# Attention and an MLP on one core: a Newton step and a scaling given to GpSimd, with a new table of half slots

## The chip, the core and the metric

The kernel runs on one core of a Trainium2 chip. The core has a matrix engine (PE; PEld is its loading of weights), two engines for elementwise work that read the matrix engine's result banks (VectorE, called DVE, and ScalarE, called ACT), GpSimd (POOL), which works on the on-chip memory SBUF alone, and SyncE (SP), which issues the transfers here. Each engine takes its instructions strictly in the order in which they were written for it. The metric is device microseconds (us) of one execution; of several runs the median counts.

## What is computed

Attention of 8 batches, 12 heads, 448 positions and 64 channels, with q and k normalised first, and behind it an MLP with exp(h) − 1 for negative h:

```python
q_n, k_n = (rmsnorm(q, g_q), rmsnorm(k, g_k))      # x / sqrt(mean(x*x) + 1e-6) * g
scores = scale * np.matmul(q_n, k_n.transpose(0, 1, 3, 2))
scores = scores - np.max(scores, axis=-1, keepdims=True)
attn = np.exp(scores)
attn = attn / (np.sum(attn, axis=-1, keepdims=True) + 1e-09)
out = np.matmul(attn, v)                           # (8, 12, 448, 64)
x = out.transpose(0, 2, 1, 3).reshape(3584, 768)
h = x @ w_in                                       # 768 -> 2048
g = np.where(h > 0.0, h, np.exp(np.minimum(h, 0.0)) - 1.0)
y = g @ w_out                                      # 2048 -> 768
```

## The kernel before

**Tiles.** Two heads make a pair: 48 pairs, six to a batch. A pair has 896 rows of scores, seven tiles of 128 rows, 336 tiles in all. Matrix products run in 16-bit halves: a number is split into a high and a low part, and two or three products are added in one bank. The weights are converted inside the kernel, in the first two batches: w_in in 16 pieces (`conv_in`), w_out in 24 (`conv_out`). In both, DVE joins bits (L243) and puts the sign back (L267), ACT makes two copies (L237, L238) and a high part (L327), POOL scales (L291, L322) and subtracts (L331).

**The way of q and k of a pair.** `load_qk`, `qk_square` (ACT, L372), `qk_sum` (DVE, L376), `qk_root` (ACT, L380 and L381: r0 = exp(−0.5 ln(mean))), `qk_newton` (DVE, lines 384 to 393 of the source: one Newton step that sharpens r0, four instructions on 14 columns that the trace has on L387 twice, L388 and L391), `qk_norm` (POOL, L401), the split into halves (ACT L410 and L420, POOL L424 and L431), and transfers that transpose it.

**The way of a tile.** `s_mm` (PE, L554) writes the scores into a bank; `s_max` (DVE, L561); `s_exp` (ACT, L575), with the sum as by-product; `s_z` (POOL, L579), one column: adds the small constant to the sum; `s_rec` (DVE, L587), its reciprocal; `s_hi` (ACT, L618, or L612) and `s_lo` (DVE, L628, or L625) write both halves of the weights of the values; then a transfer, or for the pairs 1, 3 and 5 a product with a diagonal (POOL L591, PE L599), turns them. The banks of scores are used in a ring of five, later of four, so `s_mm` waits until `s_lo` of an earlier tile is done.

**The MLP.** `mlp` yields one matrix product after the other (first layer L743, second layer L757). Behind the 18 products of one of 16 blocks of h, `m1_out` finishes the block in five steps, one slot apart: `one` (ACT, L682, exp of the bank), `two` (ACT, L686, e·isc − isc), `three` (DVE, L690, minimum and maximum against the bank), `four` (ACT, L695) and `five` (DVE, L698), which write the two halves of g.

**What sets the order.** The order on every engine is written out by the program: time is cut into slots h, two to a tile, and the table `SCHED` says in which slot (or half slot) each step of each pair, weight piece, batch and tile is written. The row "rate" says how many products of the MLP have been written by slot 85, 92, 99 and so on. Pairs from the twelfth on repeat the last row; so do batches.

Of the kernel before, what the change touches and what calls it, by code (L numbers as in the profile page):

```python
# [13 lines left out]
AF = mybir.ActivationFunctionType  # L14
ALU = mybir.AluOpType
# [4 lines left out]
B, H, S, D = 8, 12, 448, 64  # L20
# [3 lines left out]
NJ = 2 * S // 128  # L24
# [8 lines left out]
def tile_attention_then_elu_mlp(ctx: ExitStack, tc: tile.TileContext, qk, v, v_scan, gg, w_in, w_out, out):  # L33
# [13 lines left out]
    nc = tc.nc  # L47
# [19 lines left out]
    def t_mo():  # L67
# [10 lines left out]
        out=neg, in0=ident, scalar1=-1.0, scalar2=None, op0=ALU.mult  # L78
# [3 lines left out]
        out=ident, in0=ident, scalar1=2.0**UP, scalar2=None, op0=ALU.mult  # L82
# [103 lines left out]
    kap = const.tile([128, 1], F32, name="kap")  # L186
# [196 lines left out]

    def qk_newton(p):
        ss, r0 = st1[p]
        for x, op0, op1 in ((D * 1e-6, ALU.add, ALU.mult), (-0.5 / D, ALU.mult, ALU.mult)):
            nc.vector.scalar_tensor_tensor(out=ss, in0=ss, scalar=x, in1=r0, op0=op0, op1=op1)  # L387
        nc.vector.scalar_tensor_tensor(  # L388
            out=r0, in0=ss, scalar=1.5, in1=r0, op0=ALU.add, op1=ALU.mult
        )  # L390
        nc.vector.tensor_scalar(  # L391
            out=r0[:, NJ:], in0=r0[:, NJ:], scalar1=kap, scalar2=None, op0=ALU.mult
        )
# [171 lines left out]
    def by_pe(T):  # L565


        return T // NJ in PE_PAIRS
# [19 lines left out]

    def s_diag(T):
        dg = dgs[T] = pool.tile([128, 128], F32, tag="dgz", name="dgz", bufs=2)  # L590
        (nc.vector if DIAG_DVE else nc.gpsimd).tensor_scalar(  # L591
            out=dg, in0=ident, scalar1=stats[T][:, 2:3], scalar2=0.0, op0=ALU.mult, op1=ALU.add
        )

# [78 lines left out]
    def m1_out(b, f, ph):  # L673

        sc, isc, nisc, gsc = (t[:, f : f + 1] for t in mscale[b][:4])
        e = None
        g = gts[f]

        def one():
            nonlocal e  # L680
            e = pool.tile([128, S], F32, tag="e", name="e", bufs=3)
            nc.scalar.activation(e, ph[:, :S], AF.Exp, scale=sc)  # L682

        def two():

            nc.scalar.activation(e, e, AF.Identity, scale=isc, bias=nisc)  # L686

        def three():

            nc.vector.scalar_tensor_tensor(  # L690
                out=e, in0=e, scalar=0.0, in1=ph[:, :S], op0=ALU.min, op1=ALU.max
            )

        def four():
            nc.scalar.activation(g[:, 0], e, AF.Copy, scale=gsc)  # L695

        def five():
            nc.vector.scalar_tensor_tensor(  # L698
                out=g[:, 1], in0=e, scalar=gsc, in1=g[:, 0], op0=ALU.mult, op1=ALU.subtract
            )  # L700

        return [one, two, three, four, five]
# [79 lines left out]
    def put(hs, steps):  # L782
        for h, (fn, *args) in zip(hs, steps, strict=True):
            at(h, fn, *args)

    at(-18, gains)
    for T in reversed(range(NCHUNK)):
        k = 2 if by_pe(T) else 0 if T < PB else 1
        hs = [2 * T + h for h in SCHED["tile"][k]]
        j = T % NJ  # L790
        if k < 2:
            put(hs[:6], [(fn, T) for fn in (s_max, s_exp, s_z, s_rec, s_hi, s_lo)])


            at(hs[7 if j == 0 else 8 if j == NJ - 1 else 6], s_tr, T)
        else:
            put(hs, [(fn, T) for fn in (s_max, s_exp, s_z, s_rec, s_diag, s_pe, s_hi, s_lo)])
    for p in range(NP):
        k = p if p < 12 else 11
        put([h + HP * (p - k) for h in SCHED["qk"][k]], [  # L800
# [8 lines left out]
    for b in range(B):  # L809
        k = min(b, 2)  # L810
        hs = [h + HB * (b - k) for h in SCHED["scan"][k]]
# [7 lines left out]
    for b in range(B):  # L819
        k = min(b, 1)  # L820
        hs = [h + HB * (b - k) for h in SCHED["m"][k]]
# [22 lines left out]
    for h in range(H0, LAST):  # L844
        T, odd = divmod(h, 2)
# [9 lines left out]
        p, r = divmod(h, HP)  # L855
# [23 lines left out]
    for h in range(h + 1, h + 9):  # L879
# [3 lines left out]

SCHED = {
# [13 lines left out]
    ],  # L898
    "v": [
        [-2, 14, 15, 17, 18, 23, 24],  # L900
        [17, 23, 24, 24, 26, 36, 37],
        [26, 37, 38, 38, 40, 50, 51],
        [41, 52, 53, 54, 55, 65, 65],
        [54, 65, 66, 68, 68, 78, 79],
        [68, 79, 80, 82, 82, 93, 93],
        [82, 93, 94, 96, 96, 106, 106],
        [96, 107, 109, 109, 110, 120, 121],
        [110, 121, 122, 123, 124, 134, 135],
        [124, 135, 136, 137, 138, 147.5, 148.5],
        [138, 149, 150, 151, 152, 162, 162],  # L910
        [152.5, 163.5, 164.5, 165.5, 166.5, 176.5, 177.5],
    ],
    "scan": [
# [3 lines left out]
    ],  # L917
# [17 lines left out]
    ],  # L935
# [25 lines left out]
    ],  # L961
    "m": [
        [68, 69, 70, 72, 73, 74, 75, 77],
        [153, 154, 155, 156, 158, 159, 160.5, 161.5],
    ],
    "tile": [
# [3 lines left out]
    ],  # L970
    "rate": [
        [4, 8, 46, 104, 148, 188, 240, 288, 336, 382, 430, 478, 536, 576],
    ],
}
WO_OWN = 7

CK = S // 4
PE_PAIRS = (1, 3, 5)
DIAG_DVE = False

RATE_FROM = 85
UP = 13
# [38 lines left out]
```

## Time and profile before

| what | value |
|---|---|
| median of 3 runs | 1270.25 us (1269.4 to 1272.03) |
| the profiled execution's own time | 1268.82 us |
| its span, first to last instruction | 1267.0 us |
| PE busy | 1196.3 us (94%) |
| DVE busy | 861.1 us (68%) |
| ACT busy | 880.6 us (70%) |
| POOL busy | 535.4 us (42%) |

Busy time is the time in which an engine has at least one instruction in work. The shares are means over a kernel with different stages, so the table alone does not say what bounds it: the page's 40 slices (31.7 us each) show PE at 3 to 8 tenths in the first seven slices and at 9 or more from the eighth on, and DVE at 7 to 9 or more in the first eight and at 5 to 8 in most of the later ones. A wait row names who waited, for whom, for how long in total, how often, and the longest.

### The profile page before, as it was taken

Reading aid. Unit: us, or ns where it says so; the run is one execution under the profiler, and the core shown is the slowest. Engines: PE = TensorE matmul, PEld = TensorE weight load, DVE = VectorE, ACT = ScalarE, POOL = GpSimd, SP = SyncE. Lnnn points to the kernel's source line nnn. Section 1 sums busy time; section 2 is a strip of 40 time slices with the busy share of each in tenths; the row PEclk is TensorE's granted clock in tenths of the full one; section 3 lists DMA queues with packets and bytes.
Section 4 is the critical chain, followed back from the end, with each engine's and each line's share of the span. In section 5 each row is a group of like instructions: output and inputs, shape, how many; then the busy total and the mean of one; then the engine's idle time right before and its main releaser. Section 6 shows DMA issues by size and latency. Waiting matters only on the chain.

```text
span 1267.0 us, 21793 instructions
## 1 busy us (share of the span) xinstructions
PE 1196.3 (94%) x7150; PEld 735.0 (58%) x7150; DVE 861.1 (68%) x1913; ACT 880.6 (70%) x1889; POOL 535.4 (42%) x858
## 2 busy tenths in 40 slices
PE   3778678999999999999999999999999999999998
PEld 2435444567556665576556755666557755676576
DVE  7888999986676567755785667756876677642310
ACT  6888789975797568855896578756886579643520
POOL 4766877664434343433434433334334333320000
PEclk9889799999999999999999999999999999999999
DMA  9967799999677986689577976798677968672012
GB/s 296 252 154 188 197 205 201 221 215 227 155 160 151 218 177 156 145 195 215 137 162 160 237 149 158 153 220 186 144 154 184 223 140 157 137 156 76 1 49 63
DMA packets 432979, 214.44 MB, mean 169 GB/s; under 512 B 389089, under 2 KB 409185, under 8 KB 432865
## 3 DMA queue, kind: packets, MB, share of 16 engines
q1 hardware_dynamic: 432864, 213.04, 74.1%
q8 instruction: 57, 0.93, 0.3%
q14 instruction: 58, 0.47, 0.1%
HBM read 93.52 MB, written 14.16 MB: 85 GB/s over the span
## 4 chain that ended last, share of the span: by engine, by line
PE 82%; DVE 10%; ACT 3%; POOL 3%; issue 1%; DMA 1%; SPq 0%; ACTq 0%; POOLq 0%
PE m L757 23%; PE m L743 20%; PE s L757 11%; PE s L743 10%; PE s L554 9%; PE av L658 7%; DVE w32s L267 2%; DVE st L561 1%; DVE wts L243 1%; DVE gall L698 1%; DVE p L628 1%; DVE ss L376 1%; DMA raws<-in_w_out 1%; PE s L599 1%; PE m L298 1%
## 5 line engine op out<-in xcount | busy, mean ns | idle before, releaser
L561 DVE TENSOR_REDUCE st<-s 128x1 f32<-128x448 f32 x336 | 208.3, 620 | 208.4 <-PE s L554 207.1
L579 POOL TENSOR_SCALAR st<-st 128x1 f32<-128x1 f32 x336 | 85.0, 253 | 496.7 <-ACT s L575 478.6
L743 PE MATMUL m<-x,whi 128*128 128x448 f16 x1020 | 281.9, 353 | 1.0 <-DVE x L669 1.0
L757 PE MATMUL m<-gall,whos 128*128 128x448 f16 x1024 | 282.2, 353 | 0.0
L757 PEld LDWEIGHTS <-whos 128*128 128x128 f16 x1536 | 221.5, 145 | 73.6 <-issue 1.1
L618 ACT ACTIVATE p<-s,st 128x448 f16<-128x448 f32 x294 | 185.9, 632 | 84.4 <-DMA pt<-p 51.1
L575 ACT ACTIVATE s<-s,st 128x448 f32<-128x448 f32 x315 | 190.5, 605 | 62.3 <-DVE st L561 62.1
L743 PEld LDWEIGHTS <-whi 128*128 128x128 f16 x1536 | 149.3, 98 | 136.1 <-issue 1.1
L628 DVE SCALAR_TENSOR_TENSOR p<-s,st,p 128x448 f16<-128x448 f32 x294 | 198.6, 676 | 14.0 <-ACT p L618 13.8
L554 PE MATMUL s<-qkt 128*128 128x448 f16 (+1 forms) x768 | 186.4, 363 | 19.6 <-DVE gall L625 11.2
L757 PE MATMUL m<-gall,wls 128*128 128x448 f16 x512 | 181.1, 354 | 0.0
L743 PE MATMUL m<-x,wli 128*128 128x448 f16 x510 | 179.8, 353 | 0.0
L743 PE MATMUL s<-x,whi 128*128 128x448 f16 x516 | 141.7, 352 | 0.0
L757 PE MATMUL s<-gall,whos 128*128 128x448 f16 x512 | 141.2, 353 | 0.0
L757 PEld LDWEIGHTS <-wls 128*128 128x128 f16 x768 | 110.6, 144 | 41.4 <-issue 6.5
L743 PEld LDWEIGHTS <-wli 128*128 128x128 f16 x768 | 75.1, 98 | 76.1 <-issue 8.4
L698 DVE SCALAR_TENSOR_TENSOR gall<-e,gsc,gall 128x448 f16<-128x448 f32 x128 | 98.5, 769 | 24.1 <-ACT gall L695 24.1
L554 PEld LDWEIGHTS <-qkt 128*128 128x128 f16 (+1 forms) x768 | 62.6, 101 | 86.0 <-issue 45.1
L658 PE MATMUL av<-pt,vt 128*64 128x448 f16 x990 | 102.0, 354 | 1.0 <-DVE most L145 1.0
L695 ACT ACTIVATE gall<-e,gsc 128x448 f16<-128x448 f32 x128 | 85.2, 666 | 18.1 <-DVE e L690 17.7
L686 ACT ACTIVATE e<-e,nisc,isc 128x448 f32<-128x448 f32 x128 | 97.1, 758 | 0.3
L665 ACT ACTIVATE x<-av 128x448 f16<-128x448 f32 x48 | 26.0, 542 | 96.1 <-PE av L658 70.1
(120 smaller groups left out, 1778.7 us busy)
## 6 DMA issues: line engine op xcount, KB each, us to landing
wls<-wl_d SPq DMA_DIRECT2D x48, 512.0 KB, 4.2
nat<-in_qk SPq DMA_DIRECT2D x48, 448.0 KB, 3.6
raws<-in_w_out SPq DMA_DIRECT2D x24, 512.0 KB, 4.9
qkt<-qkt SPq DMA_DIRECT2D x96, 112.0 KB, 2.3
out<-y SPq DMA_DIRECT2D x48, 224.0 KB, 2.8
vn<-in_v SPq DMA_DIRECT2D x38, 256.0 KB, 3.4
vscan<-in_v_scan SPq DMA_DIRECT2D x36, 224.0 KB, 4.0
whos<-in_w_in SPq DMA_DIRECT2D x10, 768.0 KB, 6.7
```

The lines of the kernel that those rows point to most:

```text
L554: nc.tensor.matmul(ps[r0 : r0 + n, :S], lhs, qq[:, 1, h * S : h * S + S], start=(t == 0), stop=(t == 2),)
L561: nc.vector.tensor_reduce(out=st[:, 0:1], in_=pss[T][:, :S], axis=AX.X, op=ALU.max, negate=True)
L575: nc.scalar.activation(e, ps, AF.Exp, bias=st[:, 0:1], accum_out=st[:, 1:2])
L579: nc.gpsimd.tensor_scalar(out=st[:, 1:2], in0=st[:, 1:2], scalar1=1e-9, scalar2=2.0 ** (UP - 7) if by_pe(T) else 2.0**-7, op0=ALU.add, op1 ...
L618: nc.scalar.activation(p16[:, :S], pss[T][:, :S], AF.Copy, scale=stats[T][:, 2:3])
L628: nc.vector.scalar_tensor_tensor(out=p16[:, S:], in0=ps[:, :S], scalar=r, in1=p16[:, :S], op0=ALU.mult, op1=ALU.subtract)
L658: nc.tensor.matmul(av[64 * h : 64 * h + 64, :S], vs[:, h], ps[h], start=(k == 0), stop=(k == len(terms) - 1),)
L686: nc.scalar.activation(e, e, AF.Identity, scale=isc, bias=nisc)
L695: nc.scalar.activation(g[:, 0], e, AF.Copy, scale=gsc)
L698: nc.vector.scalar_tensor_tensor(out=g[:, 1], in0=e, scalar=gsc, in1=g[:, 0], op0=ALU.mult, op1=ALU.subtract)
L743: nc.tensor.matmul(ph[:, :S], w[:, c, :], x[:, r, :], start=(c == 0 and i == 0), stop=last)
L757: nc.tensor.matmul(py[:, :S], w, g[:, r, :], start=(f == 0 and i == 0), stop=last)
```

## The change

The change has three parts. `qk_newton` of the pairs 2 to 11 (counted from 0) is done by POOL in six instructions in place of four on DVE; the pairs 0, 1 and 12 to 47 keep the four. Step `two` of the MLP's 16 blocks of the first batch is done by POOL, as (e − 1)·isc; later batches keep ACT. The table of slots has new numbers. A switch that was false (`DIAG_DVE`) is gone, and a fourth row in "tile" is read by nothing.

```diff
     def qk_newton(p):
         ss, r0 = st1[p]
+        if p in NEWTON_POOL:
+            ts, tt = nc.gpsimd.tensor_scalar, nc.gpsimd.tensor_tensor
+            ts(out=ss, in0=ss, scalar1=D * 1e-6, scalar2=-0.5 / D, op0=ALU.add, op1=ALU.mult)
+            tt(out=ss, in0=ss, in1=r0, op=ALU.mult)
+            tt(out=ss, in0=ss, in1=r0, op=ALU.mult)
+            ts(out=ss, in0=ss, scalar1=1.5, scalar2=1.0, op0=ALU.add, op1=ALU.mult)
+            tt(out=r0, in0=ss, in1=r0, op=ALU.mult)
+            ts(
+                out=r0[:, NJ:], in0=r0[:, NJ:], scalar1=kap, scalar2=0.0, op0=ALU.mult,
+                op1=ALU.add,
+            )
+            return
...
         def two():
 
-            nc.scalar.activation(e, e, AF.Identity, scale=isc, bias=nisc)
+            if b in TWO_POOL:
+                nc.gpsimd.tensor_scalar(
+                    out=e, in0=e, scalar1=-1.0, scalar2=isc, op0=ALU.add, op1=ALU.mult
+                )
+            else:
+                nc.scalar.activation(e, e, AF.Identity, scale=isc, bias=nisc)
...
     "rate": [
-        [4, 8, 46, 104, 148, 188, 240, 288, 336, 382, 430, 478, 536, 576],
+        [2, 4, 46, 98, 142, 186, 238, 288, 334, 388, 428, 478, 536, 576],
     ],
...
-DIAG_DVE = False
+NEWTON_POOL = range(2, 12)
+TWO_POOL = (0,)
```

On DVE at the eleventh pair's Newton step, before (p is a tile's weights, s a bank of scores, e a block of h, wts and w32s a piece of w_out):

```order
L151 TENSOR_SCALAR ws<-most 128x1
L690 SCALAR_TENSOR_TENSOR e<-e,m_73 128x448
L628 SCALAR_TENSOR_TENSOR p_2501<-s_68,st,p_2501 128x448
L387 SCALAR_TENSOR_TENSOR ss<-ss,r_2429 128x14 x2
L388 SCALAR_TENSOR_TENSOR r_2429<-ss,r_2429 128x14
L391 TENSOR_SCALAR r_2429<-r_2429,kap 128x7
L587 RECIPROCAL st<-st 128x1
L561 TENSOR_REDUCE st<-s_67 128x1
L243 SCALAR_TENSOR_TENSOR wts<-wts,w32s 128x512
L698 SCALAR_TENSOR_TENSOR gall<-e,gsc,gall 128x448
```

The same place on DVE in the changed kernel, where lines stand 12 to 17 further down (L640 is `s_lo`, L599 `s_rec`, L573 `s_max`, L707 and L715 steps `three` and `five`):

```order
L151 TENSOR_SCALAR ws<-most 128x1
L715 SCALAR_TENSOR_TENSOR gall<-e,gsc,gall 128x448
L640 SCALAR_TENSOR_TENSOR p_2512<-s_68,st,p_2512 128x448
L599 RECIPROCAL st<-st 128x1
L243 SCALAR_TENSOR_TENSOR wts<-wts,w32s 128x512
L707 SCALAR_TENSOR_TENSOR e<-e,m_73 128x448
L573 TENSOR_REDUCE st<-s_67 128x1
L267 SCALAR_TENSOR_TENSOR w32s<-raws,wts 128x512
```

The four instructions between a tile's `s_lo` and the next reciprocal are gone; the steps around them changed places among themselves.

On POOL at the same pair, before (L579 is `s_z`, L450 scales a pair's values):

```order
L331 TENSOR_TENSOR w32s<-w32s,whos 128x512
L579 TENSOR_SCALAR st<-st 128x1
L322 TENSOR_SCALAR w32s<-w32s,ws 128x512
L450 TENSOR_SCALAR whos<-whos,vs 128x512
L331 TENSOR_TENSOR w32s<-w32s,whos 128x512
L579 TENSOR_SCALAR st<-st 128x1
```

And on POOL in the changed kernel (L699 is step `two`, L388 to L393 the Newton step, L591 `s_z`, L462 the scaling of the values):

```order
L591 TENSOR_SCALAR st<-st 128x1
L331 TENSOR_TENSOR w32s<-w32s,whos 128x512
L699 TENSOR_SCALAR e<-e,isc 128x448
L388 TENSOR_SCALAR ss<-ss 128x14
L389 TENSOR_TENSOR ss<-ss,r_2438 128x14
L390 TENSOR_TENSOR ss<-ss,r_2438 128x14
L391 TENSOR_SCALAR ss<-ss 128x14
L392 TENSOR_TENSOR r_2438<-ss,r_2438 128x14
L393 TENSOR_SCALAR r_2438<-r_2438,kap 128x7
L591 TENSOR_SCALAR st<-st 128x1
L322 TENSOR_SCALAR w32s<-w32s,ws 128x512
L462 TENSOR_SCALAR whos<-whos,vs 128x512
```

Between two `s_z` there now stand a subtraction, step `two` and the six instructions of the Newton step.

## Rows read from the trace of the kernel before

**Rows 1.** Stretches: start:end, length, busy PE, PEld, DVE, ACT, POOL; clock, DMA.
```profile
20.00:120.00 100.00, 75.05 (x511) 45.22 (x509) 89.30 (x181) 84.34 (x188) 69.75 (x95) 0.86 0.84 212
120.00:160.00 40.00, 27.79 (x212) 18.82 (x211) 38.57 (x92) 31.74 (x72) 32.26 (x44) 0.79 0.83 197
160.00:266.00 106.00, 91.94 (x648) 52.01 (x647) 102.63 (x212) 98.48 (x208) 75.51 (x94) 1.00 0.96 207
266.00:1160.00 894.00, 894.00 (x5211) 549.46 (x5210) 597.11 (x1366) 621.21 (x1357) 351.57 (x614) 1.00 0.78 172
```

**Rows 2.** DVE's waits, 20 to 120 us: total us, times, longest us.
```profile
DVE st L587 <- POOL st L579: 2.6, 3, 1.1
...
DVE a_in L145 <- PE av L142: 0.2, 1, 0.2
```

**Rows 3.** DVE's waits, 120 to 266 us.
```profile
DVE wts L243 <- ACT w32s L238: 1.2, 4, 0.4
...
DVE st L587 <- POOL st L579: 0.7, 1, 0.7
DVE p L628 <- ACT p L618: 0.4, 1, 0.4
```

**Rows 4.** PE's waits, 20 to 266 us, two of the three longest.
```profile
PE s L554 <- DVE gall L625: 11.2, 11, 2.3
...
PE s L554 <- DVE p L628: 4.8, 4, 2.0
```

**Rows 5.** Groups of DVE's instructions, 20 to 160 us: count, busy us, mean ns, idle.
```profile
L387 DVE SCALAR_TENSOR_TENSOR ss<-ss,r 128x14 f32<-128x14 f32 x12 | 3.1, 262 | 0.2
L391 DVE TENSOR_SCALAR r<-r,kap 128x7 f32<-128x7 f32 x6 | 2.0, 341 | 0.2
L388 DVE SCALAR_TENSOR_TENSOR r<-ss,r 128x14 f32<-128x14 f32 x6 | 1.0, 175 | 0.2
```

**Rows 6.** The same view of DVE, 160 to 266 us.
```profile
L698 DVE SCALAR_TENSOR_TENSOR gall<-e,gsc,gall 128x448 f16<-128x448 f32 x16 | 16.6, 1039 | 0.0
L267 DVE SCALAR_TENSOR_TENSOR w32s<-raws,wts 128x512 uint32<-128x512 uint32 x16 | 15.6, 973 | 0.1
L243 DVE SCALAR_TENSOR_TENSOR wts<-wts,w32s 128x512 uint32<-128x512 uint32 x16 | 13.3, 829 | 0.9 <-ACT w32s L238 0.9
L387 DVE SCALAR_TENSOR_TENSOR ss<-ss,r 128x14 f32<-128x14 f32 x8 | 3.0, 373 | 0.1
L391 DVE TENSOR_SCALAR r<-r,kap 128x7 f32<-128x7 f32 x4 | 1.7, 426 | 0.1
L388 DVE SCALAR_TENSOR_TENSOR r<-ss,r 128x14 f32<-128x14 f32 x4 | 0.7, 174 | 0.1
```

**Rows 7.** The same view of ACT, 160 to 266 us: step `two`.
```profile
L686 ACT ACTIVATE e<-e,nisc,isc 128x448 f32<-128x448 f32 x16 | 12.2, 763 | 0.0
```

**Rows 8.** The same view of POOL, 160 to 266 us.
```profile
L579 POOL TENSOR_SCALAR st<-st 128x1 f32<-128x1 f32 x28 | 9.8, 348 | 17.2 <-ACT s L575 14.2 <-DMA raws<-in_w_out 1.4
...
L458 POOL TENSOR_SCALAR vt<-whos 128x512 f16<-128x512 f32 x4 | 3.2, 809 | 0.2
```

**Rows 9.** The same view of POOL, 20 to 160 us: 128 columns.
```profile
L591 POOL TENSOR_SCALAR dgz<-ident,st 128x128 f32<-128x128 f32 x21 | 10.9, 518 | 5.8 <-DVE st L587 2.8 <-PE s L599 1.6 <-PE m L299 1.4
```

**Rows 10.** POOL's longest wait, 160 to 266 us.
```profile
POOL st L579 <- ACT s L575: 14.2, 9, 2.8
```

**Rows 11.** Timeline of DVE: start us, duration us, instruction.
```profile
238.28 0.68 DVE L267 SCALAR_TENSOR_TENSOR w32s<-raws,wts 128x512 uint32<-128x512 uint32 x1
238.88 0.68 DVE L698 SCALAR_TENSOR_TENSOR gall<-e,gsc,gall 128x448 f16<-128x448 f32 x1
...
248.69 2.13 DVE L698 SCALAR_TENSOR_TENSOR gall<-e,gsc,gall 128x448 f16<-128x448 f32 x1
```

**Rows 12.** Timeline of POOL, same time, with the idle time before in brackets.
```profile
240.96 1.04 POOL L431 TENSOR_TENSOR t<-nat,t 128x448 f16<-128x448 f32 x1 [2.96 <-ACT t L420]
...
248.66 1.69 POOL L401 TENSOR_TENSOR nat<-nat,r 128x896 f32<-128x896 f32 x1
```

More of the change, by code (lines that the diff above doesn't have):

```diff
@@ L590, in s_diag @@
         dg = dgs[T] = pool.tile([128, 128], F32, tag="dgz", name="dgz", bufs=2)
-        (nc.vector if DIAG_DVE else nc.gpsimd).tensor_scalar(
+        nc.gpsimd.tensor_scalar(
             out=dg, in0=ident, scalar1=stats[T][:, 2:3], scalar2=0.0, op0=ALU.mult, op1=ALU.add
@@ L684, in two @@
         def two():
-            nc.scalar.activation(e, e, AF.Identity, scale=isc, bias=nisc)
+            if b in TWO_POOL:
+                nc.gpsimd.tensor_scalar(
+                    out=e, in0=e, scalar1=-1.0, scalar2=isc, op0=ALU.add, op1=ALU.mult
+                )
+            else:
+                nc.scalar.activation(e, e, AF.Identity, scale=isc, bias=nisc)
         def three():
@@ L796, in tile_attention_then_elu_mlp @@
         else:
-            put(hs, [(fn, T) for fn in (s_max, s_exp, s_z, s_rec, s_diag, s_pe, s_hi, s_lo)])
+            put(hs, [
+                (fn, T)
+                for fn in (s_max, s_exp, s_z, s_rec, s_diag, s_pe, s_hi, s_lo)
+            ])
     for p in range(NP):
@@ L899 @@
     "v": [
[L900 to L904, printed above, removed]
+        [-2, 14, 15, 17, 18, 24, 26],
+        [17, 23, 24, 24, 26, 37, 37],
+        [26, 37, 38, 38, 41, 52, 52],
+        [41, 52, 53, 54, 55, 65, 65.5],
+        [54, 65, 66, 68, 70, 80, 80.5],
         [68, 79, 80, 82, 82, 93, 93],
-        [82, 93, 94, 96, 96, 106, 106],
+        [81.5, 92.5, 93.5, 95.5, 95.5, 105.5, 106],
         [96, 107, 109, 109, 110, 120, 121],
@@ L909 @@
         [124, 135, 136, 137, 138, 147.5, 148.5],
-        [138, 149, 150, 151, 152, 162, 162],
+        [138.5, 149.5, 150.5, 151, 152, 162, 162],
         [152.5, 163.5, 164.5, 165.5, 166.5, 176.5, 177.5],
@@ L959 @@
         [136.5, 140.5, 141.5, 143.5, 145.5, 147.5, 147.5, 148.5, 150.5, 152.5],
[1 row of a table removed]
[1 row of a table added]
     ],
     "m": [
-        [68, 69, 70, 72, 73, 74, 75, 77],
+        [68, 69, 72, 72, 73, 75, 75, 77],
         [153, 154, 155, 156, 158, 159, 160.5, 161.5],
```

73 rows, old and new, of the table SCHED are left out of this document.

## The prediction

> **What bounds the kernel now.** I read the busy time by stretches first, since the page's means hide the stages. From 266 to 1160 us PE is busy for 894.00 of 894 us at full clock [rows 1]: nothing that the other engines save there can shorten the kernel. From 20 to 266 us it is otherwise: PE is busy for 75.05 of 100, 27.79 of 40 and 91.94 of 106 us, so it stands idle for 24.9 + 12.2 + 14.1 = 51.2 us, while DVE is busy for 89.30, 38.57 and 102.63 us [rows 1]. Next I read DVE's waits. From 20 to 120 us there are seven kinds with 9.5 us in all, the longest 2.6 us and the last 0.2 us [rows 2]; from 120 to 266 us four kinds with 3.1 us, from 1.2 down to 0.4 us [rows 3]. So DVE has a queue that is hardly ever empty, and PE's waits name DVE as the one who comes last: 11.2 and 4.8 us for a bank of scores that DVE still has to read [rows 4]. The bound up to 266 us is DVE's queue, and a microsecond taken from it moves forward the moment from which PE is full. PE's work up to that moment stays the same: the rate row has 288 products of the MLP at slot 134 before and after, and 382 against 388 at slot 148. The tail is not touched.
>
> **Newton off DVE.** Ten pairs, 2 to 11, fall between 20 and 266 us: six before 160 us, four behind. Six cost 3.1 + 2.0 + 1.0 = 6.1 us busy and 0.6 us idle between them [rows 5], 6.7 us; four cost 3.0 + 1.7 + 0.7 = 5.4 and 0.3 us [rows 6], 5.7 us. That is 12.4 us off DVE's queue. Behind 120 us DVE all but never waits, so I count all of it; between 20 and 120 us a tenth of the time is waiting, so of the four pairs there I count nine tenths: 6.3 us of the 6.7.
>
> **What POOL pays.** No row shows a POOL instruction on 14 columns. The nearest are one column at 348 ns [rows 8] and 128 columns at 518 ns [rows 9]; 14 is near one, I take 0.37 us, and 0.05 us between dependent ones, as before each of the four L458 (0.2 us idle) [rows 8]. Six make 2.5 us a pair (ends 2.1 and 3.4): 10 us for the four pairs behind 160 us, 15 us for the six before. Step `two` on POOL has 448 columns; 512 columns take 809 ns and one column 348 [rows 8]; it is nearest to the first, I take 0.75 us, so 16 × 0.75 = 12.0 us (ends 5.6 and 13). Behind 160 us POOL then has 75.5 + 12.0 + 10.0 = 97.5 us of work [rows 1] in 106 us less what is saved. Before 160 us it has 69.75 + 32.26 + 15 = 117 of 140 us. So there is room, but behind 160 us only 8.5 us of it. What covers the added work is POOL's idle time: 14.2 us of waiting for exp in front of `s_z` [rows 10].
>
> **ACT.** 16 times 763 ns, 12.2 us, leave ACT [rows 7], which is busy for 98.48 of 106 us [rows 1]. I cost it at nothing: DVE, with 102.63, is the one that PE waits for, and DVE waits for ACT only a little over 2 us there [rows 3]. If ACT's queue holds up more than these rows say, it is a gain of 1 or 2 us.
>
> **DVE and POOL get in each other's way.** L267 and L698 take 0.68 us at 238.28 and 238.88, while POOL sits idle up to 240.96; L698 takes 2.13 us at 248.69, 30 ns behind the start of a POOL instruction of 1.69 us [rows 11, 12]. So a DVE instruction with two SBUF inputs waits out the POOL instruction in front of it. On average the three large groups take 1.039, 0.973 and 0.829 us [rows 6] where 0.68 would do: 16 × (0.359 + 0.293 + 0.149) = 12.8 us lost behind 160 us, for 75.5 us of POOL work, 0.17 us for each. Step `two` adds 12.0 us of such work: 12.0 × 0.17 = 2.0 us back to DVE. The Newton instructions are short; they cost between nothing and 25 × 0.17 = 4.3 us; I take a quarter, 0.6 us before 160 us and 0.4 us behind. The Trainium skill states this rule: SBUF — State Buffer, § Who interferes with whom, says that a VectorE instruction with two SBUF inputs contends with a GpSimd one that reads SBUF, and that whoever issues first holds the shared pair for the whole instruction. The two 0.68 us and the 2.13 us agree with it. By its wording a short holder costs at most its own short length, which speaks for the low end of the Newton term; with that term at nothing the time below would be 1.0 us lower.
>
> **The new wait.** `s_z` now stands behind a subtraction, `two` and six Newton instructions where a subtraction alone, or two scalings and one, stood. If it is late, `s_rec` waits, and behind it DVE's whole queue; ACT's `s_hi` and PE's next tile wait for that in turn. Before, this wait is 2.6 us in 20 to 120 us [rows 2], and a single one of 0.7 us behind it [rows 3]. Behind 160 us it can grow by nothing, or by up to the whole of what POOL is late; I take 1.2 us, 0.3 us for each of four pairs. The table's other moves, half a slot to two slots each, I cost at nothing: they reorder steps that all sit in the same full queue; their ends are the waits that they may open or close, some 4 us either way, close to half of the 9.5 us [rows 2].
>
> **The sum.** Before 160 us 6.3 − 0.6 = 5.7 us; behind it 5.7 − 2.0 − 0.4 − 1.2 = 2.1 us; together 7.8 us. The profiled execution took 1268.8 us, 1.8 us more than its span of 1267.0; less 7.8 that is 1261.0. The median of the three runs lies 1.4 us above it, so I predict **1262.4 us**. With the ends of the terms this case reaches from 1258 (12.4 us, nothing given back) to 1267 (the port term of `two` at 13 × 0.17 = 2.2, that of the Newton step at 4.3 and the new wait at 2.2 leave 12.0 − 8.7 = 3.3).
>
> **Rivals.**
> *POOL takes DVE's place, and the time stays.* With the upper ends POOL has 75.5 + 13 + 13.6 = 102 us of work behind 160 us, in an order that it can't change, and it still must wait for exp at nine places [rows 10]; if a third of these 14.2 us stays, it is full at 107 us, and nothing is saved there. Before 160 us some 2 us are left. 1268 to 1271 us. For it: the whole of POOL's spare time is claimed at once. Against it: ACT, lighter by 12.2 us, gives exp sooner. The Trainium skill names this way out: Perfetto Trace Analysis, § Optimizing Scalar/DVE Operations, says that moving work between GpSimd and VectorE might not help because they share a read port. The 0.17 us for each us alone would leave a gain, so by the rows it takes the full queue as well.
>
> *Slower: `two` at the head of POOL's queue.* Before, a late block of h held up ACT; now POOL stands still until ACT's exp of the block is there, with `s_z` of the tiles behind it, and DVE's `three` and reciprocals wait for both. It decides from the point where `two` waits for more than the 14.2 / 9 = 1.6 us that `s_z` now waits for on average [rows 10], at most of the 16 blocks. With 0.8 us lost on DVE at each, 16 × 0.8 = 12.8 us against the 7.8 saved: 1275 us. Against it: behind 160 us no wait of DVE for a block of h is among the longer ones [rows 3].
>
> *The clock stays low for longer.* PE is granted 0.79 of full clock between 120 and 160 us and 1.00 from there on [rows 1]. If the low stretch reaches 20 us further, products there at half speed cost 10 us: 1262.4 + 10, or 1272 us and a little more.
>
> *More than the Newton step.* If nothing is given back and the table closes 4 of the 9.5 us [rows 2], it is 12.4 + 4 = 16.4 us: 1254 us.
>
> **Chances.** Main case 0.60; POOL full 0.17; slower by `two` 0.08; clock 0.03, which lies on the line between no change and slower; more 0.12. A measurement of this kernel can tell about 0.2%, 2.5 us, from no change. Faster by more than that, below 1267.7: 0.60 + 0.12 + a little of the second, 0.74. Within: 0.16, the rest of the second and a part of the clock's. Slower: 0.10. The range leaves out the slower cases (0.11 with all of the clock's) and half of "more" (0.06): 1256 to 1271 us.
>
> **What would show it.** In the profile after: no Newton group on DVE between the second and the thirteenth pair; DVE's busy time up to the point at which PE is full shorter by about 9 us, and that point near 258 us in place of 266; step `two` on POOL at 0.7 to 0.8 us and the six small ones near 0.4 us; `five`, L267 and L243 a little slower on average than 1.04, 0.97 and 0.83 us; the wait of `s_rec` for `s_z` not above 5 us up to there. I am wrong if DVE shows new waits for POOL of 6 us and more, if PE still has idle time in stretches behind 266 us, or if the low clock reaches beyond 160 us.

## The result and the profile after

The changed kernel takes 1276.78 us (median of 4 runs, 1275.48 to 1277.93); the kernel before took 1270.01 us beside it. The ratio is 1.0046, interval 1.0031 to 1.0061: the change makes the kernel slower by 0.5%. The forecast was 1262.4 us and a range up to 1271; the time lies outside of it, and on the other side.

The stretches of the kernel after, columns as in [rows 1]:

```profile
20.00:120.00 100.00, 73.67 (x539) 45.09 (x539) 88.79 (x172) 87.09 (x195) 78.25 (x121) 0.93 0.86 220
120.00:160.00 40.00, 28.27 (x194) 19.31 (x191) 33.83 (x78) 30.14 (x67) 36.62 (x55) 0.70 0.75 180
160.00:266.00 106.00, 89.03 (x601) 48.34 (x601) 98.09 (x183) 83.47 (x179) 90.06 (x127) 0.98 0.87 200
...
280.00:300.00 20.00, 19.03 (x115) 13.51 (x112) 13.69 (x40) 12.03 (x29) 12.96 (x21) 1.00 0.94 201
300.00:1160.00 860.00, 860.00 (x5005) 526.41 (x5004) 570.75 (x1308) 600.27 (x1311) 332.74 (x586) 1.00 0.77 171
```

PE is full from 300 us on, not from 266 [rows 1]. Up to 300 us it stands idle for 26.3 + 11.7 + 17.0 + 1.0 = 56.0 us; before, it was 51.2 us. That is 4.8 us, and PE's own busy time is 1198.0 us in place of 1196.3. Together 6.5 us, which is the difference of the two spans (1273.5 and 1267.0 us). The clock that PE is granted is lower from 120 to 160 us (0.70 where it was 0.79) and from 160 to 266 us (0.98 for 1.00), but higher from 20 to 120 us (0.93 for 0.86); how much of the 1.7 us comes from the clock is not shown. DVE's busy time did get shorter: by 9.8 us up to 266 us (230.5 before, 220.7 after), of which 7.4 us are left over the whole execution (861.1 and 853.7), since some of its work now lies behind 266 us. In its place stands waiting: DVE's waits from 20 to 266 us are 23.2 us in all, where they were 12.6. Waits of DVE, first from 20 to 120 us, then from 120 to 266 us; then one row of ACT's from 120 to 266 us; last, one of PE's from 20 to 290 us:

```profile
DVE st L599 <- POOL st L591: 5.3, 4, 2.0
...
DVE st L599 <- POOL st L591: 6.5, 7, 2.9
DVE gall L715 <- ACT gall L712: 4.3, 4, 1.4
...
ACT whos L327 <- POOL w32s L322: 15.8, 10, 2.9
...
PE s L611 <- POOL dgz L603: 8.6, 8, 3.1
```

The reciprocal's wait for `s_z` was 2.6 us [rows 2] and 0.7 us [rows 3]; now it is 11.8 us in all. ACT's wait for POOL's scaled piece of w_out is the longest of ACT there. PE waits for the diagonals that POOL builds (dgz) for 8.6 us, where it was 2.9 before. POOL itself has 90.06 us of work in the 106 us from 160 on, and its wait for exp there is down from 14.2 us [rows 10] to

```profile
POOL st L591 <- ACT s L587: 4.5, 4, 2.1
```

One place shows how it happens. Where the longest of the reciprocal's waits lies, the timeline of POOL, columns as in [rows 11, 12]:

```profile
140.21 2.15 POOL L436 TENSOR_TENSOR t<-nat,t 128x448 f16<-128x448 f32 x1
142.34 0.37 POOL L603 TENSOR_SCALAR dgz<-ident,st 128x128 f32<-128x128 f32 x1
142.79 0.21 POOL L388 TENSOR_SCALAR ss<-ss 128x14 f32<-128x14 f32 x1
...
144.31 0.29 POOL L393 TENSOR_SCALAR r<-r,kap 128x7 f32<-128x7 f32 x1
144.68 0.19 POOL L591 TENSOR_SCALAR st<-st 128x1 f32<-128x1 f32 x1
```

The timeline of DVE, then a row of ACT's, at the same place:

```profile
141.38 0.61 DVE L573 TENSOR_REDUCE st<-s 128x1 f32<-128x448 f32 x1
144.90 0.16 DVE L599 RECIPROCAL st<-st 128x1 f32<-128x1 f32 x1 [2.91 <-POOL st L591]
```

```profile
140.36 0.19 ACT L587 ACTIVATION_READ_ACCUMULATOR ex<-s,st 128x1 f32 x1
```

The tile's sum was there at 140.55 us. `s_z`, 0.19 us long, started at 144.68, behind a subtraction of 2.15 us, a diagonal and the six Newton instructions (142.79 to 144.60 us). DVE stood still for 2.91 us, and 1.9 us of that are the time of the Newton step that had been taken off it.

### The profile page after: what moved, and what is told of

It is laid out like the page before. It is cut to its first block, busy times and chain, and to the rows that moved or that the text cites. A ratio compares the mean times of both kernels' runs of the same rounds, so it can differ in the third digit from the quotient of the medians.

```text
span 1273.5 us, 21835 instructions
## 1 busy us (share of the span) xinstructions
PE 1198.0 (94%) x7150; PEld 735.6 (58%) x7150; DVE 853.7 (67%) x1873; ACT 870.8 (68%) x1873; POOL 567.7 (45%) x934
## 4 chain that ended last, share of the span: by engine, by line
PE 78%; POOL 1%; DVE 1%; ACT 1%; DMA 1%; issue 0%; ACTq 0%; POOLq 0%
PE m L774 22%; PE m L760 20%; PE s L774 11%; PE s L760 10%; PE s L566 8%; PE av L670 6%; DMA pt<-p 1%; POOL w32s L331 0%; DVE gall L715 0%; POOL w32s L322 0%; DVE p L640 0%; POOL e L699 0%; ACT p L630 0%; ACT s L587 0%; ACT gall L712 0%
## 5 line engine op out<-in xcount | busy, mean ns | idle before, releaser
L573 DVE TENSOR_REDUCE st<-s 128x1 f32<-128x448 f32 x336 | 208.6, 621 | 203.6 <-PE s L566 202.3
L591 POOL TENSOR_SCALAR st<-st 128x1 f32<-128x1 f32 x336 | 87.7, 261 | 479.0 <-ACT s L587 464.7
L640 DVE SCALAR_TENSOR_TENSOR p<-s,st,p 128x448 f16<-128x448 f32 x294 | 199.0, 677 | 22.2 <-ACT p L630 22.0
L715 DVE SCALAR_TENSOR_TENSOR gall<-e,gsc,gall 128x448 f16<-128x448 f32 x128 | 100.6, 786 | 28.9 <-ACT gall L712 28.7
L760 PE MATMUL s<-x,wli 128*128 128x448 f16 x258 | 91.0, 353 | 0.0
L774 PE MATMUL s<-gall,wls 128*128 128x448 f16 x256 | 90.6, 354 | 0.0
```

The costliest lines, as they stand in the source:

```text
L573: nc.vector.tensor_reduce(out=st[:, 0:1], in_=pss[T][:, :S], axis=AX.X, op=ALU.max, negate=True)
L591: nc.gpsimd.tensor_scalar(out=st[:, 1:2], in0=st[:, 1:2], scalar1=1e-9, scalar2=2.0 ** (UP - 7) if by_pe(T) else 2.0**-7, op0=ALU.add, op1 ...
L640: nc.vector.scalar_tensor_tensor(out=p16[:, S:], in0=ps[:, :S], scalar=r, in1=p16[:, :S], op0=ALU.mult, op1=ALU.subtract)
L715: nc.vector.scalar_tensor_tensor(out=g[:, 1], in0=e, scalar=gsc, in1=g[:, 0], op0=ALU.mult, op1=ALU.subtract)
L760: nc.tensor.matmul(ph[:, :S], w[:, c, :], x[:, r, :], start=(c == 0 and i == 0), stop=last)
L774: nc.tensor.matmul(py[:, :S], w, g[:, r, :], start=(f == 0 and i == 0), stop=last)
```

## The experiments

In what follows "table" is the new table of slots. Times are medians; differences between kernels are differences of the ratios to the kernel before, which ran beside each, times 1270 us. Single intervals are 0.1 to 0.17% either way, so a difference of two kernels is known to 2 to 3 us either way, and one below that is not told from nothing.

| kernel | Newton, pairs 2 to 11 | `two`, first batch | `s_z`, tiles below 84 | us | ratio, interval |
|---|---|---|---|---|---|
| after | POOL | POOL | POOL | 1276.8 | 1.0046 (1.0031 to 1.0061) |
| old_both (table of before) | POOL | POOL | POOL | 1280.3 | 1.0073 (1.0058 to 1.0088) |
| new_none | DVE | ACT | POOL | 1267.1 | 0.9971 (0.9957 to 0.9985) |
| new_newton | POOL | ACT | POOL | 1272.8 | 1.0006 (0.9997 to 1.0015) |
| new_two | DVE | POOL | POOL | 1270.8 | 1.0000 (0.9990 to 1.0010) |
| new_nonewton | left out | ACT | POOL | 1264.0 | 0.9952 (0.9936 to 0.9969) |
| new_notwo | DVE | left out | POOL | 1267.3 | 0.9973 (0.9963 to 0.9984) |
| new_extra6 | DVE, and six more on POOL | ACT | POOL | 1274.4 | 1.0032 (1.0021 to 1.0044) |
| new_dve4 | DVE, and four more on DVE | ACT | POOL | 1277.9 | 1.0053 (1.0038 to 1.0068) |
| after_z_act | POOL | POOL | ACT | 1268.0 | 0.9977 (0.9968 to 0.9987) |
| none_z_act | DVE | ACT | ACT | 1264.5 | 0.9948 (0.9933 to 0.9962) |
| newton_z_act | POOL | ACT | ACT | 1263.6 | 0.9941 (0.9924 to 0.9957) |
| extra6_z_act | DVE, and six more on POOL | ACT | ACT | 1267.4 | 0.9966 (0.9954 to 0.9978) |
| nonewton_z_act | left out | ACT | ACT | 1259.1 | 0.9909 (0.9895 to 0.9924) |
| nonewton_notwo | left out | left out | POOL | 1262.3 | 0.9934 (0.9917 to 0.9951) |
| nonewton_z_act_notwo | left out | left out | ACT | 1256.4 | 0.9892 (0.9877 to 0.9906) |

### Which part costs

The changed kernel with a part undone. In old_both it is the table: the numbers of the kernel before are put back. In the others it is a step's engine:

```diff
-NEWTON_POOL = range(2, 12)
-TWO_POOL = (0,)
+NEWTON_POOL = ()
+TWO_POOL = ()
```

This is new_none; new_newton has the second line of it alone, new_two the first.

new_newton: 

> The changed kernel with step two of the MLP's first batch given back to ACT: only the Newton step and the new table are left of the change. Theory A (POOL's queue is full from about 140 us on, and whatever is added to it comes back as waiting): 14 us of work leave POOL behind 160 us, most of the loss goes, 1264 to 1269 us. Theory B (the new table itself costs the time): 1276 us or more. Theory C (step two at the head of POOL's queue is the whole cost): the forecast gain of the Newton step shows, 1262 us.

new_two: 

> The changed kernel with the Newton step of the pairs 2 to 11 given back to DVE: only step two and the new table are left. Theory A: POOL has 12 to 14 us more than before from 172 to 260 us and DVE nothing less: 1271 to 1276 us, slower than before, not slower than the whole change. Theory B: DVE has its 12 us again on top of a bad table, 1285 us. Theory C: 1280 us or more, since the gain of the Newton step is gone and the cost of step two stays.

new_none: 

> The new table alone, with both steps where they were before. Theory A: the table alone changes little, 1268 to 1273 us. Theory B: the table is the loss, 1277 us or more. Theory C says nothing against 1270 us.

old_both: 

> Both steps on POOL with the table of before. Theory A: POOL has the same work as in the changed kernel, 1275 to 1282 us, and the new table had moved some steps out of the way. Theory B: without the new table the moves gain, 1262 us. Theory C: 1275 us.

The table alone gains 3.7 us, and with both steps moved it still gains 3.4 (old_both against after). So the table is not the cause (theory B). On it the Newton step on POOL costs 4.4 us, `two` on POOL 3.7, both 9.5. Neither is the whole of it (theory C); each of the two steps is a loss of its own. Theory A has the place, POOL's queue, but of its ranges only that of old_both holds. new_newton missed it by nearly 4 us: the Newton step alone costs more than A left for it. new_two and new_none came out just below their ranges.

### What DVE's relief is worth, and what POOL's work costs

All three stand on the table alone. In new_nonewton, against the changed kernel, nothing is left of the step for these pairs:

```diff
         ss, r0 = st1[p]
         if p in NEWTON_POOL:
-            ts, tt = nc.gpsimd.tensor_scalar, nc.gpsimd.tensor_tensor
...
-            tt(out=r0, in0=ss, in1=r0, op=ALU.mult)
...
             return
```

In new_extra6 the six instructions of the change work on two scratch tiles, sp and s0, that were set to 1 before, and the four of DVE follow as before the change:

```diff
+            tt(out=sp, in0=sp, in1=s0, op=ALU.mult)
...
+            tt(out=s0, in0=sp, in1=s0, op=ALU.mult)
...
-            return
```

In new_notwo:

```diff
-            else:
+            elif b:
                 nc.scalar.activation(e, e, AF.Identity, scale=isc, bias=nisc)
```

new_nonewton: 

> The new table with step two on ACT, and the Newton step of the pairs 2 to 11 left out altogether: DVE is relieved and nobody pays. The reference is the new table alone (1267 us). Theory A (DVE was the bound, as the prediction had it, and POOL's queue took the gain back): about 12 us less, 1255 to 1258 us. Theory D (DVE was full but not alone the bound; the other queues and the clock are right behind it): 3 us less at most, 1264 to 1267 us.

new_extra6: 

> The new table with both steps where they were before, and six more instructions on POOL for each of the pairs 2 to 11, on 14 columns of a tile of their own that nobody reads: POOL pays and DVE is not relieved. The reference is the new table alone (1267 us). Theory A: what POOL gets in its queue comes back, 10 us or more on top of 1267, since the Newton step on POOL lost 5.7 us although DVE had 12 us less: 1275 to 1280 us. Theory D: it costs what the real one costs, about 5 us: 1271 to 1274 us.

new_notwo: 

> The new table with the Newton step on DVE, and step two of the first batch's MLP left out altogether: ACT has 12 us less and nobody pays. The reference is the new table alone (1267 us). Theory A: nothing, 1265 to 1268 us, since DVE has as much as before. Theory D: ACT is as close to the bound as DVE, 1261 to 1264 us.

The two halves of the Newton step's move, taken apart: 12 us off DVE's queue bring 2.4 us (new_nonewton against new_none; the interval reaches from nothing to 5 us, near theory D's 3 and far from theory A's 12), and the six instructions on POOL, with nobody reading what they write, cost 7.7 us, between the ranges of theories A and D. The sum, 5.3 us of loss, is near the 4.4 that the move itself costs. ACT's 12 us are worth nothing while the rest stays, as theory A had it. From 20 to 290 us, new_none, then new_extra6:

```profile
DVE st L599 <- POOL st L591: 1.9, 1, 1.9
ACT whos L327 <- POOL w32s L322: 2.2, 4, 0.8
```
```profile
DVE st L602 <- POOL st L594: 5.9, 7, 1.2
ACT whos L327 <- POOL w32s L322: 6.7, 9, 1.7
```

Nobody waits for what the six instructions write. Two ways are left for their price: what stands behind them in POOL's queue comes later, or they slow DVE's instructions down, as the port term of the prediction has it. The second is not seen: DVE's busy time over the whole execution is 859.6 us in new_none and 859.5 in new_extra6. So it is the queue: `s_z`, the pieces of w_out and the diagonals, for which PE waits 8.9 us in place of 3.7.

### The way on which it reaches the others

`s_z` is one column wide. In the next four kernels ACT computes it in the tiles below 84, right behind its own exp; everything else stays where it is. This does two things at once: `s_z` no longer waits in POOL's queue, and that queue gets shorter, by 79 steps of 25.7 us in all (new_none, 20 to 290 us).

```diff
+        if T < 2 * PB:
+            c = 2.0 ** (UP - 7) if by_pe(T) else 2.0**-7
+            nc.scalar.activation(st[:, 1:2], st[:, 1:2], AF.Copy, scale=c, bias=c * 1e-9)
+            return
```

after_z_act: 

> The changed kernel with the one-column step between a tile's exp and its reciprocal done by ACT in place of POOL for the first two batches (84 tiles), so that it no longer stands in POOL's queue. Theory A: the loss came through the reciprocal that waits for this step; the waits of DVE for POOL go, and the change gains what was forecast, 1262 to 1267 us. Theory D: the loss comes through all that POOL hands on (the scaled weights too), and ACT pays some 15 us for 84 small steps: 1273 us or more.

none_z_act: 

> New table, both steps at their old places (as in new_none, 1267.1 us), and s_z, the scaling of a tile's row sum, computed by ScalarE instead of GpSimd in the tiles below 84. In new_none the reciprocal s_rec waited for s_z only 1.9 us between 20 and 290 us. Theory A (GpSimd's queue delays s_z only through the work that the change adds): nothing to gain here, 1265 to 1268. Rival E (the hand-over of s_z through GpSimd costs something in every tile, with the added work or without it, so that the gain of after_z_act against the changed kernel was this and not the removal of the added work's price): about the same 8 us as there, 1258 to 1261.

newton_z_act: 

> New table, Newton step by GpSimd from the third pair on, `two` left on ScalarE, and s_z by ScalarE in the tiles below 84. Against new_newton (1272.8 us). Theory A with s_z as the only way on which GpSimd's lateness reaches DVE: the price goes and the 2.5 to 3 us that new_nonewton showed as the worth of DVE's relief come forward, 1263 to 1266. Rival F (GpSimd's lateness goes on by its other products as well, q's and k's turn, dgz and the weights' w32s, on which PE and ScalarE wait): part of it stays, 1267 to 1271.

extra6_z_act: 

> As new_extra6 (Newton step on DVE as before, and GpSimd computes the same six small operations in each of ten pairs a second time on tiles that nobody reads; 1274.4 us), with s_z by ScalarE in the tiles below 84. Theory A with s_z as the only way: GpSimd's six operations cost nothing then, 1266 to 1268, as none_z_act. Rival F: as much as 4 to 7 us stays, 1271 to 1274.

Against its twin with `s_z` on POOL, each gains: after 8.8 us, extra6 8.4, newton 8.3, none 2.9. So `s_z` out of POOL's queue is worth 2.9 us with no added work there, where theory A had nothing and rival E 8, and 5.4 us more once the Newton instructions are there. newton_z_act and extra6_z_act came out in theory A's ranges, after_z_act 1 us above. Of the 7.7 us that six instructions on POOL cost, 2.3 are left (extra6_z_act against none_z_act), which is within the intervals. With that, the Newton step on POOL turns from a loss of 4.4 us into a gain of 0.9, also within the intervals. How much of this is `s_z` coming earlier, and how much the shorter queue, no run tells: ACT's wait for the pieces of w_out falls too, from 7.4 us in new_newton to 1.5 in newton_z_act. PE's wait for the diagonals stays high, though, from 20 to 290 us in newton_z_act:

```profile
PE s L615 <- POOL dgz L607: 8.3, 6, 3.6
```

It is as long there as in the changed kernel, which takes 13 us more, so it does not set the difference. Step `two` on POOL is another matter: with the Newton step on POOL it costs 5.1 us with `s_z` on POOL (after against new_newton) and 4.6 without (after_z_act against newton_z_act). Its price goes another way; newton_z_act, then after_z_act, ACT's waits from 20 to 290 us, and DVE's group of step `five` from 160 to 266 us:

```profile
ACT whos L327 <- POOL w32s L322: 1.5, 3, 0.7
...
L719 DVE SCALAR_TENSOR_TENSOR gall<-e,gsc,gall 128x448 f16<-128x448 f32 x16 | 16.0, 1002 | 0.2 <-ACT gall L716 0.2
```
```profile
ACT whos L327 <- POOL w32s L322: 9.6, 10, 1.9
...
L719 DVE SCALAR_TENSOR_TENSOR gall<-e,gsc,gall 128x448 f16<-128x448 f32 x16 | 18.3, 1144 | 3.0 <-ACT gall L716 3.0
```

With `two` on POOL, ACT waits 8.1 us more for the weights' pieces, DVE's `five` takes 2.3 us more in all and waits 2.8 us more for ACT. These rows lie where the price must be; no run took one of them away alone, so how the 4.6 us are shared among them is open.

### Why DVE's relief is worth so little

On the table alone, ahead of the step's own four instructions, four more on scratch tiles:

```diff
+        if 2 <= p < 12:
+            for x, op0, op1 in ((D * 1e-6, ALU.add, ALU.mult), (-0.5 / D, ALU.mult, ALU.mult)):
+                nc.vector.scalar_tensor_tensor(out=sp, in0=sp, scalar=x, in1=s0, op0=op0, op1=op1)
+            nc.vector.scalar_tensor_tensor(
+                out=s0, in0=sp, scalar=1.5, in1=s0, op0=ALU.add, op1=ALU.mult
+            )
+            nc.vector.tensor_scalar(
+                out=s0[:, NJ:], in0=s0[:, NJ:], scalar1=kap, scalar2=None, op0=ALU.mult
+            )
```

new_dve4: 

> New table, both steps at their old places, and DVE computes four more small operations of the Newton step's kinds and sizes in each of the ten pairs from the third on, on tiles that nobody reads: about 1.05 us a pair up to 160 us (twice 0.320, 0.174 and 0.232 us), 11 to 12 us in all. The step of the prediction under question is that a microsecond on DVE's queue is a microsecond of the start of the full stretch of TensorE. If that holds upwards: 1267 plus 9 to 12, 1276 to 1279. Theory D (DVE is full but one of several limits that lie close together, as new_nonewton gave back only 2.4 to 3.3 of 12 us): a bound that is only just the bound gives little when relieved but charges the whole when loaded, so 1274 to 1279 as well; if DVE has slack of its own that its waits hide, 1268 to 1271.

The four instructions of ten pairs, sp and s their scratch tiles, 20 to 290 us:

```profile
L404 DVE SCALAR_TENSOR_TENSOR sp<-sp,s 128x14 f32<-128x14 f32 x20 | 6.2, 310 | 0.4
L408 DVE TENSOR_SCALAR s<-s,kap 128x7 f32<-128x7 f32 x10 | 2.3, 231 | 0.4
L405 DVE SCALAR_TENSOR_TENSOR s<-sp,s 128x14 f32<-128x14 f32 x10 | 1.7, 174 | 0.3
```

10.2 us busy and 1.1 us between them cost 10.4 us: upwards the prediction's step, a microsecond on DVE for a microsecond of the kernel, holds. Theory D has the same range there, so this run speaks only against slack on DVE. Downwards the step does not hold: in new_nonewton DVE's waits for `s_z` from 20 to 290 us rise to 4.8 us, from the 1.9 of new_none:

```profile
DVE st L589 <- POOL st L581: 4.8, 6, 1.2
```

What is next behind DVE was asked with three kernels that leave out the Newton step and relieve a second and a third queue:

nonewton_z_act: 

> New table, Newton step of the ten pairs 2 to 11 left out, s_z by ScalarE in the tiles below 84. Theory G (GpSimd's queue, through s_z, is the limit right behind DVE): DVE's relief comes forward once this one is gone too, 1253 to 1258. Theory H (it is another limit): near new_nonewton's 1264.0 and newton_z_act's 1263.6, 1260 to 1264.

nonewton_notwo: 

> New table, Newton step of the ten pairs left out, and `two` (exp(h) - 1 scaled) of the first batch's MLP left out of ScalarE's work. Relieves DVE of 12 us and ScalarE of 12 us, GpSimd of nothing. Theory I (ScalarE is the limit right behind DVE; alone its relief was worth nothing, as DVE stood before it): well under new_nonewton's 1264.0, 1253 to 1258. Theories G and K (clock and hand-overs): 1261 to 1264.

nonewton_z_act_notwo: 

> New table, Newton step of the ten pairs left out, `two` of the first batch's MLP left out, s_z by ScalarE in the tiles below 84: all three queues relieved at once. Theory K (TensorE's own work in its slow clock and the hand-overs from engine to engine within a tile set the time once the queues are relieved by a few us): 1259 to 1263. Theories G and I, or the two together: 1250 to 1257.

DVE's 12 us alone bring 2.4 us, with `s_z` off POOL 5.0 (nonewton_z_act against none_z_act), and ACT's 12 us, worth nothing alone, bring 2.3 on top of new_nonewton and 2.2 on top of nonewton_z_act, each within the intervals. The three reliefs one by one make 2.4 + 2.9 − 0.3 = 5.0 us; all at once they make 10.0. That no single one of them gives the 10.0 us is clear of the noise; that together they give more than their sum is not, since 5.0 us is what five intervals make together. nonewton_z_act's 1259.1 us lies between the ranges of G and H, nonewton_notwo's 1262.3 misses I's, and K, which gave 1259 to 1263 for all three at once, falls with 1256.4 us. So no theory names one successor; the rows fit DVE, POOL's `s_z` and ACT standing one close behind the other, but do not put them in order. Part of the gain of new_nonewton was also given back by PE: new_none, then new_nonewton, from 20 to 160 us:

```profile
20.00:120.00 100.00, 75.21 (x531) 46.58 (x531) 91.46 (x186) 85.60 (x194) 70.85 (x96) 0.90 0.84 218
120.00:160.00 40.00, 25.95 (x205) 17.37 (x202) 38.35 (x91) 32.89 (x73) 35.54 (x46) 0.83 0.85 198
```
```profile
20.00:120.00 100.00, 76.58 (x552) 46.62 (x550) 91.65 (x175) 87.71 (x198) 72.50 (x98) 0.90 0.89 223
120.00:160.00 40.00, 26.05 (x183) 17.04 (x182) 35.01 (x83) 32.80 (x75) 36.27 (x47) 0.74 0.87 198
```

PE got through 736 products in 101.2 us and through 735 in 102.6, with a granted clock of 0.74 in place of 0.83 behind 120 us. Over the whole profiled execution its busy time grew from 1196.7 to 1198.5 us and its idle time fell from 1265.3 − 1196.7 = 68.6 to 1262.0 − 1198.5 = 63.5 us: 5.1 us were gained and 1.8 given back. That is one execution of each, and it is no rule: the faster nonewton_z_act has 1191.7 us of PE's busy time.

The fastest kernel that computes all of it is newton_z_act: 1263.6 us, 0.9941 (0.9924 to 0.9957) of the kernel before, and against the changed kernel 1.05% less. It keeps the table and the Newton step on POOL, leaves `two` on ACT and gives `s_z` to ACT. none_z_act (1264.5) is not told from it.

## Why the prediction was wrong

**The bound.** That PE is short of work up to some 266 us and full from there holds in the traces above, with 300 us as the latest moment. That DVE's queue is the bound holds upwards (new_dve4). The failing step is "a microsecond taken from it moves forward the moment from which PE is full": the 12.0 us counted are worth 2.4 us on this table, and on POOL the six instructions cost 7.7. Busy shares and few waits show that an engine is loaded, not how far behind it the next one stands. The rows gave a hint of it, no more: ACT's 98.48 us of 106 stood in the same row as DVE's 102.63 [rows 1], a distance of 4 us, and the forecast took 5.7 us off DVE there; but the change takes 12 us off ACT as well.

**What POOL pays.** The sizes were near: six instructions take 10.3 us and 3.1 us between them for six pairs (forecast 15), and 7.5 + 2.0 us for four (forecast 10). Groups of POOL in the kernel after: two of the six from 20 to 160 us, and step `two` from 160 to 266 us.

```profile
L393 POOL TENSOR_SCALAR r<-r,kap 128x7 f32<-128x7 f32 x6 | 2.3, 382 | 0.6
...
L388 POOL TENSOR_SCALAR ss<-ss 128x14 f32<-128x14 f32 x6 | 1.3, 214 | 0.5
...
L699 POOL TENSOR_SCALAR e<-e,isc 128x448 f32<-128x448 f32 x16 | 14.0, 874 | 2.4 <-ACT e L694 2.0
```

Between the small ones lie 0.08 us, where 0.05 had been taken. `two` takes 14.0 us, 2.0 over the forecast and 1.0 over its end. The claim that failed is what covers it: "POOL's idle time". An in-order queue has idle time in the mean, and still whatever stands behind the added work is late by it wherever there is none at that place. Before 160 us, where the sum said "there is room" (117 of 140 us), lies the longest of the reciprocal's waits, at 142 to 145 us.

**The new wait.** Its place was named, `s_z` behind the moved work, and so was the sign to look for ("not above 5 us"; it is 11.8 us). Its price, 1.2 us, is the term that was mis-sized most: the wait grew by 8.5 us, and the runs with and without `s_z` in that queue differ by 5.4 us more once the Newton instructions are there, in which the shorter queue may have a share. I gave it only to the four pairs behind 160 us, and none to the six before.

**ACT.** Costed at nothing, and new_notwo shows it: nothing. The reason given then, that DVE alone is waited for, may be only half of it: with DVE relieved ACT's 12 us bring 2.3, which is within the intervals.

**The port.** `five`, L267 and L243 from 160 to 266 us, in the kernel after:

```profile
L715 DVE SCALAR_TENSOR_TENSOR gall<-e,gsc,gall 128x448 f16<-128x448 f32 x16 | 17.8, 1110 | 4.3 <-ACT gall L712 4.3
...
L243 DVE SCALAR_TENSOR_TENSOR wts<-wts,w32s 128x512 uint32<-128x512 uint32 x15 | 16.1, 1073 | 0.4 <-ACT w32s L238 0.4
...
L267 DVE SCALAR_TENSOR_TENSOR w32s<-raws,wts 128x512 uint32<-128x512 uint32 x15 | 14.0, 934 | 0.1
```

Against [rows 6] that is 16 × 0.071 + 15 × 0.244 − 15 × 0.039 = 4.2 us, where 2.0 + 0.4 had been put. The table alone, without added work on POOL, moves these means too (0.950 us for `five`, 0.868 for L243, 1.047 for L267 in new_none); against it, it is 3.9 us. The sum was about 2 us too small; that all of it is the port is not shown, since L267 got faster. Like the new wait, this term gives back to DVE some of what had been taken off it.

**The table.** At nothing, with ends of 4 us; it gains 3.7.

**The rivals.** "POOL takes DVE's place" had the mechanism and the wrong price: it let the time stay, while POOL's lateness costs more than DVE's relief brings. The section of the Trainium skill named there (Perfetto Trace Analysis, § Optimizing Scalar/DVE Operations) says that such a move might not help, for the shared read port; the move did not help, but the larger part of its price went with `s_z` out of POOL's queue (9.5 us with it, 3.7 without, after_z_act against none_z_act), though the moved instructions stayed on POOL. "`two` at the head of POOL's queue" had the sign and 1275 us, close to the time, but not the cause: POOL waits three times, 2.0 us in all, for exp before `two`, where the rival needed more than 1.6 us at most of the 16 blocks, and `two` is 3.7 to 5.1 of the 9.5 us. The low clock did reach beyond 160 us, as one of the signs of being wrong had it: 0.91 from 160 to 180 us, where it was 1.00. But new_none has 0.83 there and is faster than the kernel before, and PE's busy time grew by 1.7 us, not by 10.

## What to carry to other kernels

Before an instruction goes to an engine "with room", look at what stands behind it in that engine's queue and who waits for that: here a result of one column, 0.19 us long, came late from POOL, and DVE stood still for it. What relief of an engine is worth is found by leaving its work out, not from its busy share; adding work tells the other side only (here 10.4 us up for 11 us, 2.4 us down for 12). In this kernel it paid to take the small operation that others wait for out of the queue that gets the added work: 8.3 to 8.8 us with the Newton instructions on POOL, 2.9 without.

## What the runs showed of the hardware

- Small instructions on POOL can take less than the rows of before suggested: 14 columns 0.21 to 0.22 us in the timeline at 143 us, and the single column of `s_z` 0.19 us, where its mean was 348 ns [rows 8]. In the mean they take more: 0.21 to 0.43 us for 14 columns in the kernel after. Between dependent ones lie about 0.08 us (0.5 us for six). ACT's `s_z` takes 0.20 us, as its group in none_z_act from 20 to 290 us shows:

```profile
L593 ACT ACTIVATE st<-st 128x1 f32<-128x1 f32 x80 | 16.1, 201 | 0.6
```

- ACT carries these 16.1 us in the stretch where it was taken for nearly full, and the kernel still gets faster by 2.9 us: what a step adds to its engine's load counted for less than what POOL's queue gains without it.
